# Infini-attention with a gated FFN on one core: a new instruction order, planned with turns for the readers of one PSUM bank

## The chip, the core and the metric

The kernel runs on one core of one Trainium2 chip. The core has five instruction streams that run side by side and wait for each other by semaphores: TensorE (PE in the profile; PEld is its weight load), VectorE (DVE), ScalarE (ACT), GpSimd (POOL) and SyncE (SP), which issues nearly all DMAs. Products of TensorE land in PSUM, which this kernel uses as eight banks of 128 x 512 floats. The metric is the device time of one execution in microseconds; shown are the median and the extremes of three runs, and one more execution that was profiled.

## What is computed

The input is 2048 tokens of width 512. There are 32 heads of width 16, and the tokens are four segments of 512. Cut to its core, the reference is:

```
x = A_x
h = x + A(layernorm(x))
out = h + B(layernorm(h))

A: q, k, v = x @ wq, x @ wk, x @ wv, per head
   for each of four segments s, in order:
       a_dot = softmax(qs ks^T * scale + causal mask) vs
       a_mem = phi(qs) M / (phi(qs) z + 1e-6),   phi(t) = t+1 if t > 0 else exp(t)
       o = g * a_mem + (1 - g) * a_dot,          g = sigmoid(beta)
       M += phi(ks)^T vs;  z += sum of phi(ks)
   return concat(o) @ wo
B: (gelu(x @ w_gate) * (x @ w_up)) @ w_down      # hidden width 1376
```

All of it is float32. TensorE gets each operand as a high part in a rounded format and the low rest, and forms three products (high x high, high x low, low x high); so almost every operand needs a copy (the high part) and a subtraction (the low part) on ACT, DVE or POOL before TensorE may use it.

## The kernel before

**Stages.** The attention runs in 16 units, each one segment and one group of eight heads. A unit normalises and transposes its segment (once per segment), projects q and k (L959, and L980 for the first unit), projects v (L1008, and L1021 for the first), moves q and k by DMA into the stacked tiles `stq` and `stk`, then runs a pass that finds each query's largest score (scores L1213 on PE, maxima L1223 on DVE), and a second pass that recomputes the scores transposed (L1271), takes exponentials (L1277 on ACT), masks them (L1285 on POOL) and multiplies by v (L1299). After the attention come the output projection (L1372, L1379), the second norm, and the FFN in two halves of 1024 tokens. FFN products (L1563) and most of the down projection (L1737) are done as seven block products in place of eight; the last hidden tiles of the second half go through a plain down projection, L1631, whose sums are added to the output rows (L1639 on DVE) and stored (L1644). What the seven-product part gives is transposed on DVE (L718), sent through the DRAM tensor `y_dram`, loaded again and added on POOL (L1775).

**What sets the order.** The kernel first records 5308 operations, each with an engine, a planned duration, the values it reads and the values it writes. `ORDER` is a written-out permutation of them. `Sched.run` goes through `ORDER` and emits each operation on its engine; the engines' own queues are therefore exactly the order of the list, and nothing is reordered later. Buffers (rows of `P2`, PSUM banks, operand slots of 128 x 2 x 512) are given out in the same walk: of the free buffers a value takes the one that by the planned times came free first. So the planned times choose which buffer a value gets, and through this which semaphore it waits for. Waits are put in by the framework from the tiles that the instructions really touch, not from the plan.

**The opening.** `ln1_first` (L876) loads the first segment's four row tiles (L882), takes statistics per tile (L891, L892), adds epsilon into a PSUM bank (L899), takes the root on ACT (L901), inverts (L906) and forms the shift (L907), applies both (L912 on DVE for even tiles, L916 on ACT for odd ones; the pages name tiles by buffer), transposes on PE (L921), and splits (L926 on ACT, L928 on DVE). It does so in two halves of two tiles, called the first half and the second half below. Before the first real transpose PE runs 14 small transposes of a unit matrix (L896). SP issues the loads of the first Wk and Wq (`split_weight`, L686), of Wv (`split_wv`, L703) and of the second segment's rows (L938). The low part of Wk is formed on POOL (L692), that of Wq on DVE (L695).

**The norms.** `layer_norm` (L726) has two ways to invert the root: a root on ACT (L797) with a reciprocal on DVE (L801, L802), and a series of DVE steps (L778), of which one reads a small tile `z` in SBUF twice.

**The end.** `geglu` (L1579) leaves the activated hidden tile in SBUF (`e`) or in a PSUM bank; for the last tiles its high part is taken by ACT (L1596) and its low part by POOL or DVE (L1599). `down` (L1617) cuts the last output tile of all into two halves of 256 columns, which have sums and stores of their own; the second half's store is issued by ACT.

## Time and profile before

| | before |
|---|---|
| median of 3 runs | 741.16 us (741.01 to 743.85) |
| profiled execution | 740.42 us |
| its span in the profile | 738.7 us |
| PE busy | 719.6 us of the span, 6442 instructions |
| DVE busy | 634.8 us, 1990 instructions |
| ACT busy | 534.0 us, 1138 instructions |
| POOL busy | 523.1 us, 815 instructions |
| granted TensorE clock | 1.00 |
| DMA queue of SP | 135.71 MB, packets take 63.6% of 16 engines' span |

The span is counted from the first to the last instruction of the program; 1.7 us of the execution lie around it. The profile lists idle time of each engine before a group of instructions and the instruction that ended it. Busy time of PE counts a matmul that waits inside PE's pipeline as busy, so a stretch with PE busy throughout can still hold short waits; these are then seen on PEld, whose loads wait for the operand or the bank.

### The profile page before, as it was taken

How to read it: one execution, taken by the hardware profiler on the slowest of the kernel's cores; microseconds unless marked ns; L12 is line 12 of the kernel's file. 1: busy time of each engine (PE TensorE's matmuls, PEld its weight loads, DVE VectorE, ACT ScalarE, POOL GpSimd, SP SyncE). 2: the span in 40 equal slices, each digit the busy share in tenths (PEclk: the TensorE clock that was granted, in tenths of full speed). 3: DMA queues.
4: the chain of work that ended last, by engine and by line, in shares of the span. 5: the costliest groups of instructions: out<-in, count | busy, mean ns of one | idle time of the engine just before them, and what ended most of it. 6: DMA issues, size and time to landing. Idle time of an engine off the chain costs nothing.

```text
span 738.7 us, 19243 instructions
## 1 busy us (share of the span) xinstructions
PE 719.6 (97%) x6442; PEld 570.6 (77%) x6442; DVE 634.8 (86%) x1990; ACT 534.0 (72%) x1138; POOL 523.1 (71%) x815
## 2 busy tenths in 40 slices
PE   6999999999999999999999999999999999999996
PEld 5877877777878787777666888888887778888885
DVE  6998889988988888898987665889999999779996
ACT  6789979798685878867867656978787665666341
POOL 6344253554553746778899899998999977698766
PEclk9999999999999999999999999999999999999999
DMA  7754537656666776887856267677574249756767
GB/s 256 204 144 109 131 99 191 183 142 174 170 157 168 193 202 190 210 237 202 212 189 211 74 198 234 214 238 216 185 219 142 71 127 269 247 180 204 220 173 248
DMA packets 100798, 137.32 MB, mean 186 GB/s; under 512 B 18028, under 2 KB 40732, under 8 KB 100700
## 3 DMA queue, kind: packets, MB, share of 16 engines
q1 hardware_dynamic: 100396, 135.71, 63.6%
q8 instruction: 51, 0.84, 0.5%
q10 hardware_dynamic: 304, 0.39, 0.2%
q14 instruction: 47, 0.39, 0.2%
HBM read 70.67 MB, written 39.26 MB: 149 GB/s over the span
## 4 chain that ended last, share of the span: by engine, by line
PE 67%; DVE 11%; issue 3%; POOL 2%; DMA 2%; ACT 2%; SPq 1%; ACTq 0%; DVEq 0%; POOLq 0%
PE bank L1563 23%; PE bank L959 8%; PE bank L1299 7%; PE bank L1737 7%; PE bank L1271 5%; PE bank L1213 4%; PE bank L1379 3%; PE bank L1372 3%; PE bank L1008 3%; DVE row L1748 2%; DVE aside L1223 2%; PE bank L1631 2%; DVE bank L1223 1%; PE bank L1181 1%; DMA t_dram<-row 1%
## 5 line engine op out<-in xcount | busy, mean ns | idle before, releaser
L1277 ACT ACTIVATE row<-bank 128x512 f32<-128x512 f32 x320 | 170.9, 608 | 24.8 <-PE bank L1271 20.3
L1285 POOL TENSOR_SCALAR_AFFINE_SELECT row<-row 128x256 f32<-128x256 f32 (+1 forms) x320 | 107.8, 364 | 96.1 <-ACT row L1277 95.0
L1223 DVE CUSTOM_DVE_ANT_0 aside<-bank,amask 128x256 f32<-128x256 f32 (+2 forms) x384 | 141.1, 419 | 12.4 <-PE bank L1213 6.7
L959 PE MATMUL bank<-slot,slot 64*128 64x512 f32 x720 | 113.5, 403 | 0.3 <-DVE nm L1223 0.2
L1563 PE MATMUL bank<-slot,slot 128*128 128x512 f32 (+1 forms) x366 | 97.3, 390 | 0.0
L1223 DVE CUSTOM_DVE_ANT_0 bank<-bank,amask 128x512 f32<-128x512 f32 x128 | 86.1, 710 | 10.5 <-PE bank L1213 7.5
L1271 PE MATMUL bank<-stq,stk 64*128 64x128 f32 (+3 forms) x512 | 82.1, 337 | 0.8 <-ACT row L1114 0.5
L1299 PE MATMUL bank<-row,vaug 128*32 128x512 f32 (+3 forms) x1024 | 79.0, 436 | 1.8 <-DVE nm L1223 1.2
L1213 PE MATMUL bank<-stk,stq 64*128 64x256 f32 (+3 forms) x512 | 78.9, 326 | 1.7 <-DVE nm L1223 1.1
L1563 PEld LDWEIGHTS bank<-slot,slot 128*128 128x128 f32 (+1 forms) x366 | 67.8, 186 | 15.8 <-ACT stq L1419 0.4
L1748 DVE TENSOR_TENSOR row<-row,bank 128x512 f32<-128x512 f32 x110 | 72.0, 677 | 7.1 <-PE bank L1737 5.6
L959 PEld LDWEIGHTS bank<-slot,slot 64*128 64x128 f32 x720 | 73.3, 185 | 6.0 <-DVE nm L1223 0.7
L1528 POOL TENSOR_TENSOR slot<-row,slot 128x512 fp32r<-128x512 f32 (+3 forms) x60 | 67.1, 1124 | 14.1 <-ACT slot L1526 14.0
L1271 PEld LDWEIGHTS bank<-stq,stk 64*128 64x128 f32 x512 | 55.5, 185 | 15.5 <-DVE nm L1223 3.7
L1213 PEld LDWEIGHTS bank<-stk,stq 64*128 64x128 f32 x512 | 56.1, 185 | 9.6 <-DVE nm L1223 2.4
L1737 PE MATMUL bank<-slot,half 128*128 128x512 f32 x234 | 61.7, 390 | 0.0
L1299 PEld LDWEIGHTS bank<-row,vaug 128*32 128x32 f32 x1024 | 30.0, 109 | 39.2 <-issue 34.1
L1008 PE MATMUL bank<-slot,slot 64*128 64x256 f32 x672 | 53.4, 284 | 0.0
L1570 ACT ACTIVATE vaug<-bank 128x512 f32<-128x512 f32 (+1 forms) x66 | 38.5, 591 | 18.6 <-PE bank L1563 18.5
L1737 PEld LDWEIGHTS bank<-slot,half 128*128 128x128 f32 x234 | 43.8, 188 | 9.6 <-DVE row L1748 0.4
L1223 DVE DVE_READ_ACCUMULATOR2_ANT nm<- 128x1 f32 x512 | 49.9, 97 | 0.0
L1008 PEld LDWEIGHTS bank<-slot,slot 64*128 64x128 f32 x672 | 48.7, 186 | 1.0 <-DVE mb L1138 0.2
(228 smaller groups left out, 1722.2 us busy)
## 6 DMA issues: line engine op xcount, KB each, us to landing
stq<-slot SPq DMA_DIRECT2D x96, 128.0 KB
stk<-slot SPq DMA_DIRECT2D x94, 128.0 KB
row<-x SPq DMA_DIRECT2D x32, 256.0 KB
pv_dram<-row SPq DMA_DIRECT2D x32, 256.0 KB
row<-r_dram SPq DMA_DIRECT2D x28, 256.0 KB
wd_dram<-half SPq DMA_DIRECT2D x28, 256.0 KB
half<-wd_dram SPq DMA_DIRECT2D x28, 256.0 KB
row<-wu SPq DMA_DIRECT2D x20, 256.0 KB
```

The costliest lines, as they stand in the source:

```text
L959: return nc.tensor.matmul(pm[i].t, w[i].t[rows_of(r), wi, dc * P:(dc + 1) * P], XT[s][dc].t[rows_of(r), xi, :], start=(dc, wi, xi, ph) == ...
L1008: return nc.tensor.matmul(pms[n].t[:, 256 * t:256 * t + 256], XT[s][dc].t[rows_of(r), xi, t0:t0 + P], whl[wi].t[rows_of(r), dc // 2, 256 * ...
L1213: nc.tensor.matmul(sa.t[:, c0:c0 + w], sq.t[own, p, i * P:(i + 1) * P], sk.t[own, p, 0:w], start=True, stop=True, tile_position=(64 * a, 0 ...
L1223: nc.vector.tensor_tensor_reduce(out=(sa.t[:, c0:c0 + w] if i > 2 else aside[:, turns[0]:turns[0] + w]), in0=sa.t[:, c0:c0 + w], in1=amask ...
L1271: nc.tensor.matmul(sc.t[:, c0:c0 + D - q0], sk.t[own, p, q0:q0 + P], sq.t[own, p, q0:D], start=True, stop=True, tile_position=(64 * a, 0), ...
L1277: act(w, prio, lambda sc=sc, e=e: nc.scalar.activation(e.t[:, :w], sc.t[:, :w], AF.Exp), [sc, vtab], [e])
L1285: nc.gpsimd.affine_select(v, v, pattern=pat + [[1, P]], compare_op=OP.is_ge, fill=0.0, base=0, channel_multiplier=-1)
L1299: nc.tensor.matmul(pv.t[32 * n:32 * n + 32, kb * P:D], va.t[:, 136 * kb + 17 * j:136 * kb + 17 * j + 32], e.t[:, lo:lo + D - kb * P], star ...
L1528: pool(0.14 + 2.13e-3 * (hi - lo), prio, lambda: nc.gpsimd.tensor_tensor(v.t[:, 1, :hi - lo], r.t[:, lo:hi], v.t[:, 0, :hi - lo].bitcast(F ...
L1563: nc.tensor.matmul(dst.t[:w], v.t[:, wi, c0 + j * w:c0 + (j + 1) * w], b[bk][j].t[:, xi, :], start=first and j == 0 and n == 0, stop=j == ...
L1737: nc.tensor.matmul(dst[u].t, ws[a].t[0][:, wi, P * u:P * u + P], h[bk].t[:, xi], start=first and m == 0, stop=m == 2, skip_group_check=True)
L1748: dve(D, prio, lambda u=u, acc=acc: nc.vector.tensor_tensor(acc.t, acc.t, src[u].t, op=OP.add), [src[u]], [acc])
```

## The change

The list `ORDER` is replaced whole: 5308 entries become 5309, for the operations are numbered anew. Its first line tells a reader nothing; the rows further down show what it does.

```diff
 ORDER = [
-    4, 6, 10, 76, 0, 1, 2, 5, 11, 9, 12, 7, 27, 13, 14, 8, 16, 18, 28, 100, 91, 92, 29, 15, 17, 88, 30, 31, 32, 34,
...
+    6, 4, 77, 10, 5, 11, 9, 13, 14, 15, 92, 93, 12, 8, 29, 17, 19, 16, 18, 98, 89, 99, 90, 7, 28, 91, 30, 20, 21, 31,
...
```

**The plan knows turns.** The pool of PSUM banks is marked, and in the planned times an ACT or DVE operation that reads a bank starts only after the other engine's last planned read of the same value. This changes planned times, hence which buffers come free first, and no instruction by itself. Planned sizes of loads (`kb`) and durations (`dur`) change too.

```diff
-    PD = PX = PYZ = PA = PB = PPV = Pool_(banks)
+    PD = PX = PYZ = PA = PB = PPV = Pool_(banks, turns=True)
...
+        o.reads = [v for v in ins if v.pool is not None and v.pool.turns] if eng in ("ACT", "DVE") else []
...
+            for v in o.reads:
+                for e, end in v.read.items():
+                    if e != o.eng:
+                        at = max(at, end + LAT[e][o.eng])
```

**Small operands go to PSUM.** In `ln1_first` and in the norms with a root, the root stays in the PSUM bank, a second reciprocal writes the inverse there as well, and the shift is formed from it. In the series, `z` is written to PSUM, copied once to SBUF, and the step that read `z` twice now reads one copy from each.

```diff
+        def third():
+            if scratch:
+                nc.vector.tensor_copy(z.t, z_())
+            nc.vector.scalar_tensor_tensor(u_(), z.t, -10.0 / 3.0, z_(), op0=OP.add, op1=OP.mult)
...
             def inv(two=two):
-                nc.vector.reciprocal(y.t[:, two], z.t[:, two])
-                nc.vector.scalar_tensor_tensor(b.t[:, two], mv.t[:, two, 0], -1.0, y.t[:, two], op0=OP.mult,
+                nc.vector.reciprocal(y.t[:, two], sc.t[:, two])
+                nc.vector.reciprocal(sc.t[:, two], sc.t[:, two])
+                nc.vector.scalar_tensor_tensor(b.t[:, two], mv.t[:, two, 0], -1.0, sc.t[:, two], op0=OP.mult,
                                                op1=OP.mult)
```

**The end.** Hidden tile 9 of the second half is left in a PSUM bank (`u_` or `g_`) in place of the SBUF tile `e`, and its split reads it there. The last output tile is no longer cut: one sum of 512 columns, one store, issued by SP.

```diff
+            if f == 9 and hh:
+                o = g_ if s else u_
...
-                parts = 2 if (p, fl, s, t) == (1, groups[-1], 1, 3) else 1
...
-                        n, q = 8 * p + 4 * s + t, nc.scalar if i else nc.sync
+                    dma(prio, lambda a=a, dst=dst: nc.sync.dma_start(dst, a.t), [a],
```

**Finer pieces.** The first unit's v projection is recorded as eight operations with one bank each in place of four with two (`plain(n, t, h)`); the unit transposes of the opening are two operations in place of one; the low part of Wv no longer waits for the second half of its high part; the loads of Wv no longer stand behind the norm in the plan. The matmuls and their number are the same but for the uncut tile.

**What moves: the loads of the opening.** On SP, the first loads of the program were, and are (`x` are token rows, the first four of which are the first segment):

```order
L882 DMA row_101<-x 128x512
L882 DMA row_104<-x 128x512
L882 DMA row_105<-x 128x512
L882 DMA row_106<-x 128x512
L686 DMA row_107<-wk 128x512
L686 DMA row_108<-wq 128x512
L938 DMA row_109<-x 128x512
L703 DMA row_111<-wv 128x512
```

```order
L897 DMA row_101<-x 128x512
L897 DMA row_102<-x 128x512
L695 DMA row_103<-wk 128x512
L897 DMA row_104<-x 128x512
L712 DMA row_105<-wv 128x512
L695 DMA row_106<-wq 128x512
L897 DMA row_107<-x 128x512
L956 DMA row_111<-x 128x512
```

Wk goes from fifth place to third, the first segment's third tile from third to fourth, its last tile from fourth to seventh; Wq stays sixth. On PE, twelve of the first unit's q and k products (L998, before L980) now stand ahead of the second half's transposes; before, all sixteen transposes came first.

**What moves: the first norm on DVE.** From the second tile's statistics on, DVE's rows of the opening were, and are (`bank` holds the root's small operands, `ln` are the small SBUF tiles):

```order
L891 BN_STATS bn_158<-row_104 128x6
L892 BN_AGGR mv_160<-bn_158 128x2
L899 TENSOR_SCALAR bank_66<-mv_160 128x2
L891 BN_STATS bn_158<-row_105 128x6
L892 BN_AGGR mv_160<-bn_158 128x2
L906 RECIPROCAL ln_163<-ln_162 128x2
L907 SCALAR_TENSOR_TENSOR ln_164<-mv_160,ln_163 128x2
L891 BN_STATS bn_158<-row_106 128x6
```

```order
L907 BN_STATS bn_158<-row_102 128x6
L908 BN_AGGR mv_160<-bn_158 128x2
L916 TENSOR_SCALAR bank_66<-mv_160 128x2
L923 RECIPROCAL ln_162<-bank_66 128x2
L924 RECIPROCAL bank_66<-bank_66 128x2
L925 SCALAR_TENSOR_TENSOR ln_163<-mv_160,bank_66 128x2
L907 BN_STATS bn_158<-row_104 128x6
L908 BN_AGGR mv_160<-bn_158 128x2
```

The first half's inverse and shift now stand ahead of the third tile's statistics, and there is one reciprocal more.

**What moves: the last rows of ACT.** Here `slot` and `stq` and `stk` are operands of the last down projection, `row` hidden tiles in SBUF; before and after:

```order
L1596 ACTIVATE slot_89<-row_124 128x512
L1596 ACTIVATE slot_78<-row_122 128x512
L1585 ACTIVATE row_127<-row_127 128x512
L1644 DMA out_dram<-row_112 128x256
L1596 ACTIVATE slot_73<-row_127 128x512
```

```order
L1618 ACTIVATE stk_91<-row_108 128x512
L1601 ACTIVATE row_114<-bank_69 128x512
L1618 ACTIVATE slot_88<-bank_68 128x512
L1605 ACTIVATE row_114<-row_114 128x512
L1618 ACTIVATE stk_94<-bank_72 128x512
```

The store of the half tile, which stood ahead of the last operand's high part, is gone from ACT, and the last two operands come from banks.

More of the change, by code (lines that the diff above doesn't have):

```diff
@@ L58, with __init__ @@
 ORDER = [
[271 rows of a table removed]
[271 rows of a table added]
 ]
 class Pool_:
-    def __init__(self, tiles, fifo=False, then=None):
+    def __init__(self, tiles, fifo=False, then=None, turns=False):
+        self.turns = turns
         self.free = [(0.0, i, t) for i, t in enumerate(tiles)]
@@ L391, in __init__ @@
         self.users = 0
+        self.read = {}
         self.until = 0.0
@@ L399 @@
     __slots__ = ("eng", "dur", "lat", "fn", "prio", "vals", "preds", "succ", "n", "ready", "idx", "head", "tail",
-                 "mode")
+                 "mode", "reads")
 LAT = {
@@ L482, in run @@
             free[o.eng] = end
+            for v in o.reads:
+                v.read[o.eng] = end
             if o.eng == "SP":
@@ L810, in layer_norm @@
             for f, ins, outs in steps:
-                dve(4, prio, f, ins, outs)
+                dve(200 if f is third and scratch else 4, prio, f, ins, outs)
         if off:
@@ L1014, in vproj, with plain @@
         parts = [(t, h) for t in range(2) for h in range(2)]
-        def plain(t, h):
-            for n in range(2):
-                for dc in (2 * h, 2 * h + 1):
-                    for i, (xi, wi) in enumerate(SPLIT):
-                        t0 = (2 * n + t) * P
-                        nc.tensor.matmul(
-                            pms[n].t[:, 256 * t:256 * t + 256], XT[s][dc].t[:, xi, t0:t0 + P],
-                            whl[wi].t[:, h, 256 * (dc % 2):256 * (dc % 2) + 256],
-                            start=dc == 0 and i == 0, stop=dc == ND - 1 and i == 2)
-        for t, h in parts if s == c == 0 else []:
-            pe(12 * mm(256), prio, lambda t=t, h=h: plain(t, h), [*whl, *xt(s, 2 * h), *xt(s, 2 * h + 1)], pms, acq=va)
+        def plain(n, t, h):
+            for dc in (2 * h, 2 * h + 1):
+                for i, (xi, wi) in enumerate(SPLIT):
+                    t0 = (2 * n + t) * P
+                    nc.tensor.matmul(
+                        pms[n].t[:, 256 * t:256 * t + 256], XT[s][dc].t[:, xi, t0:t0 + P],
+                        whl[wi].t[:, h, 256 * (dc % 2):256 * (dc % 2) + 256],
+                        start=dc == 0 and i == 0, stop=dc == ND - 1 and i == 2)
+        for n in range(2) if s == c == 0 else []:
+            for t, h in parts:
+                both = slice(2 * h, 2 * h + 2)
+                pe(6 * mm(256), prio, lambda n=n, t=t, h=h: plain(n, t, h), [*whl, *XH[n][both], *XLH[n][both]],
+                   [pms[n]], acq=[*XT[0][both]] + (va if (n, t, h) == (0, 0, 0) else []))
         if s or c:
@@ L1590, in geglu @@
             o = g_ if s and f % 2 and by7(p, f) else e
+            if f == 9 and hh:
+                o = g_ if s else u_
             dve(D, prio, lambda: nc.vector.scalar_tensor_tensor(
-                o.t[:w], r.t[:w], 0.5, u_.t[:w], op0=OP.mult, op1=OP.mult), [u_] if o is r else [u_, r], [o])
+                o.t[:w], r.t[:w], 0.5, u_.t[:w], op0=OP.mult, op1=OP.mult), [v for v in (u_, r) if v is not o], [o])
             HH[p, f, s] = hh or o
@@ L1620, in down, with dn @@
             for t in range(4):
-                parts = 2 if (p, fl, s, t) == (1, groups[-1], 1, 3) else 1
-                a, W_ = ACC[4 * s + t], D // parts
-                halves = [slice(i * W_, (i + 1) * W_) for i in range(parts)]
-                pms = [Val(PD) for _ in halves]
+                a = ACC[4 * s + t]
+                pm = Val(PD)
                 for f in fl:
-                    def dn(t=t, f=f, s=s, pm=None, cs=None):
+                    def dn(t=t, f=f, s=s, pm=pm):
                         w = FW[f]
```

86 lines of the change are left out of this document (42 added, 44 removed), and 540 rows, old and new, of the table ORDER.

## The prediction

> **What bounds the kernel now.** I read the page's first rows, then busy time by stretch, then who waited for whom, and last the timeline at the places where PE waits.
>
> ```profile
> PE 719.6 (97%) x6442; PEld 570.6 (77%) x6442; DVE 634.8 (86%) x1990; ACT 534.0 (72%) x1138; POOL 523.1 (71%) x815
> PE 67%; DVE 11%; issue 3%; POOL 2%; DMA 2%; ACT 2%; SPq 1%; ACTq 0%; DVEq 0%; POOLq 0%
> ```
>
> ```profile
> core 0: us, PE busy (x) PEld busy (x) DVE busy (x) ACT busy (x) POOL busy (x), PEclk, DMA share, GB/s
> 0.00:8.27 8.27, 3.15 (x15) 1.80 (x15) 3.72 (x12) 2.53 (x5) 4.77 (x17) 1.00 0.71 236
> 8.27:24.14 15.87, 14.14 (x112) 13.32 (x113) 13.07 (x38) 13.08 (x35) 11.32 (x20) 1.00 0.75 241
> 24.14:376.00 351.86, 346.79 (x4655) 270.88 (x4657) 310.88 (x1340) 283.01 (x637) 195.75 (x448) 1.00 0.66 175
> 376.00:390.00 14.00, 13.12 (x141) 7.72 (x137) 11.49 (x30) 11.52 (x24) 12.32 (x21) 1.00 0.47 155
> 390.00:560.00 170.00, 170.00 (x772) 137.82 (x769) 137.45 (x277) 124.53 (x257) 160.05 (x178) 1.00 0.65 201
> 560.00:580.00 20.00, 19.53 (x83) 14.74 (x82) 19.88 (x34) 14.84 (x31) 19.43 (x22) 1.00 0.35 103
> 580.00:720.00 140.00, 139.98 (x616) 114.12 (x615) 125.99 (x246) 81.23 (x151) 107.90 (x104) 1.00 0.64 193
> 720.00:738.70 18.70, 12.94 (x62) 10.21 (x60) 12.28 (x19) 3.23 (x6) 11.56 (x9) 0.99 0.75 248
> ```
>
> PE is the bound: 97% busy, 67% of the chain, and without a gap for 310 of the 330 us of FFN (390 to 720). The change leaves PE's work as it is, and the granted clock is already 1.00. So all it can win lies in five places: the opening up to the first scores at 24.14 (PE idle for 8.27 - 3.15 = 5.1 us, then 15.87 - 14.14 = 1.7 us), the attention (351.86 - 346.79 = 5.1 us idle, with more waits inside busy time), the second norm at 376 to 390 (0.9 us), the middle of the FFN (0.5 us) and the end (5.8 us, most of it draining). What the attention hides shows on the weight loads:
>
> ```profile
> PEld bank L1271 <- DVE nm L1223: 3.7, 12, 0.4
> PEld bank L1213 <- DVE nm L1223: 2.4, 6, 1.2
> PEld bank L1299 <- POOL row L1285: 1.8, 5, 0.5
> PEld bank L1271 <- ACT row L1277: 1.7, 6, 0.4
> ```
>
> These four (asked between 20 and 376 us) make 9.6 us. Each is a bank or a row that another engine has not left or made in time, so they depend on the order alone.
>
> **The end.** Before, the last products wait for the low part of the last operand:
>
> ```profile
> 723.98 8.69 POOL L1775 TENSOR_TENSOR row<-row,row 128x512 f32<-128x512 f32 x6
> ...
> 727.79 0.38 ACTq L1644 DMA_DIRECT2D out_dram<-row  x1
> 728.22 0.63 ACT L1596 ACTIVATE slot<-row 128x512 fp32r<-128x512 f32 x1 [4.13 <-DVE row L1639]
> 728.89 1.38 DVE L1599 TENSOR_TENSOR slot<-row,slot 128x512 fp32r<-128x512 f32 x1 [1.13 <-ACT slot L1596]
> 730.32 0.96 PE L1631 MATMUL bank<-stq,slot 128*128 128x512 f32 x3 [0.63 <-DVE slot L1599]
> 732.32 2.05 DVE L1639 TENSOR_TENSOR row<-row,bank 128x512 f32<-128x512 f32 x3 [0.26 <-PE bank L1631]
> ```
>
> The half tile's store sits in ACT's queue ahead of that operand's high part and holds it for 4.13 us. Without it ACT can start when its row is done, about 2 us earlier, and PE's wait of **0.63 us** goes. The uncut tile also saves one add and one store, but those overlap PE. Next to be late is POOL: six additions in 8.69 us, ending at 732.67, while the last three adds on DVE start at 732.32. In the new list POOL has eight such additions in a row at the end; at 8.69 / 6 = 1.45 us each that is 11.6 us, and they must start before 721.1 not to be late. Their rows come back from `y_dram` as before. I take -0.6 us, between -1.0 (POOL's additions also freed) and +0.7 (POOL late by half an addition).
>
> **The second norm.** Its series on DVE holds the transposes, and one step of it is long:
>
> ```profile
> 380.27 1.28 POOL L1340 TENSOR_TENSOR row<-row,row 128x512 f32<-128x512 f32 x1
> 380.41 1.17 DVE L778 SCALAR_TENSOR_TENSOR bank<-ln 128x4 f32<-128x4 f32 x1
> 381.62 0.16 DVE L778 SCALAR_TENSOR_TENSOR ln<-bank,ln 128x4 f32<-128x4 f32 x1
> 385.09 0.28 PE L831 MATMUL bank<-ident,row 64*128 64x64 f32 x2 [0.36 <-DVE row L822]
> ```
>
> A step on 128 x 4 numbers takes 0.16 us where one operand is a bank, and 1.17 us where both are SBUF and POOL is at work: it ends when POOL does. The change gives that step one operand from each and adds a copy of about 0.17. So 1.17 becomes 0.16 + 0.17: 0.8 us less on the chain that PE's transposes wait for. PE's idle time in this stretch is 0.9 us, so I take **-0.8**, between -0.9 and 0 (another norm step meets POOL).
>
> **The opening.** Both directions occur. The first half's inverse moves ahead of the third tile's statistics:
>
> ```profile
> 5.45 0.17 ACT L901 ACTIVATE ln<-bank 128x2 f32<-128x2 f32 x1 [2.12 <-DVE bank L899]
> 6.21 0.69 DVE L891 BATCH_NORM_STATS2 bn<-row 128x6 f32<-128x512 f32 x1 [0.79 <-DMA row<-x]
> 7.04 0.13 DVE L906 RECIPROCAL ln<-ln 128x2 f32<-128x2 f32 x1
> 7.21 0.16 DVE L907 SCALAR_TENSOR_TENSOR ln<-mv,ln 128x2 f32<-128x2 f32 x1
> 7.40 0.81 ACT L916 ACTIVATE row<-row,ln,ln 128x512 f32<-128x512 f32 x1 [1.78 <-DVE ln L907]
> ```
>
> The root is there at 5.62; the reciprocal could follow at about 5.7, so the shift is ready some 1.1 us earlier, less 0.17 for the new reciprocal. But ACT now takes Wk's high part in between. In the second half the shift takes 1.08 us beside POOL and will take 0.16:
>
> ```profile
> 8.82 1.27 POOL L692 TENSOR_TENSOR slot<-row,slot 128x512 fp32r<-128x512 f32 x1 [2.94 <-ACT ln L901]
> 9.02 1.08 DVE L907 SCALAR_TENSOR_TENSOR ln<-mv,ln 128x2 f32<-128x2 f32 x1
> 8.15 0.33 SPq L686 DMA_DIRECT2D row<-wk  x1
> 8.82 0.33 SPq L938 DMA_DIRECT2D row<-x  x1
> ```
>
> Against this, the first segment's last tile is now the seventh load. The third load had landed at 6.21 (the statistics above). SP holds eight loads; its issues at 8.15 and 8.82 wait for the sixth and the seventh, some 0.65 us apart. So the last tile lands near 8.8 instead of 6.9 (8.8 less three loads), and the second half's statistics, root and shift run some 1.0 us later even with the shorter shift (1.9 - 0.9). PE has cover for part of it: twelve products of 0.125 us (48 take 6.0 us, row below) now stand ahead of the second transposes.
>
> ```profile
> L980 PE MATMUL bank<-slot,slot 128*128 128x256 f32 x48 | 6.0, 285 | 0.1
> L1021 PE MATMUL bank<-slot,slot 128*128 128x256 f32 x48 | 5.9, 283 | 0.0
> ```
>
> That is 1.5 us of cover against 1.0 us of delay. I take **0**, between -1.1 (the first half's head start kept) and +1.9 (the late tile uncovered).
>
> **The attention.** Here only the order counts. The plan now holds back an ACT read of a bank while DVE reads it. The waits are real already:
>
> ```profile
> ACT row L990 <- DVE slot L1072: 3.3, 6, 0.9
> ```
>
> That is the idle time of ACT before its read of a projected bank (L990), ended by DVE's read of the same bank (L1072). ACT is not the bound, so these 3.3 us cost PE little. What the plan gains is truer times at which banks come free, the very thing PE's loads wait for in the 9.6 us above. I take **-1.5** of it, about a sixth. Nothing in the trace excludes that other waits replace these: the ends are -4.8 (half goes) and +4.8 (they grow by half). The middle of the FFN, 0.5 us idle, I take at -0.2.
>
> The Trainium skill, page "PSUM — Partial Sum Buffer", section "PSUM bank collisions raise a hardware error", says that two engines must not access one bank in the same quadrant at once, reads included, and that the scheduler adds a dependency between them. The trace agrees: the 3.3 us are such waits. By this rule the new plan removes no wait, since each of them stands in the program either way; then the attention's term is 0, which is the second rival.
> The page "SBUF — State Buffer", section "SBUF: two separate sides", says that a DVE operation with two SBUF inputs and a GpSimd operation that reads SBUF lock each other out for the whole instruction. The 1.17 and 1.08 us beside POOL agree. By it the two norm steps are cured for good, as in my sum.
>
> **The sum.** 740.42 - 0.6 - 0.8 + 0 - 1.5 - 0.2 = 737.3 us against the profiled execution. The median of the runs shown, 741.16, is 0.7 above that execution, so the forecast for a median is **738.0 us**.
>
> **Rivals.**
> 1. *The attention gains much.* If half of the 9.6 us goes (4.8 in place of 1.5), the time is 738.0 - 3.3 = 734.7. For it: the waits are many (29) and short, 0.3 us each, so a slightly truer plan reaches them. Against it: the old order was fitted to nearly the same plan.
> 2. *The turns are bookkeeping.* The semaphores stay and waits only move, so the attention and the FFN's middle give nothing, and the late tile costs 0.9 of its 1.9 us: 738.0 + 1.7 + 0.9 = 740.6. For it: PE in attention is busy for 346.79 of 351.86 us, little is left.
> 3. *Slower: the new order makes PE's loads wait longer for banks that the maxima (L1223) or exponentials (L1277) hold.* If the four rows grow by half, that is +4.8 in place of -1.5: 738.0 + 6.3 = 744.3. It decides from the point where they grow by more than the other terms save (0.6 + 0.8 + 0.2 = 1.6 us, a sixth of 9.6); beyond that the kernel is slower than before. For it: DVE is busy for 310.88 of 351.86 us there, so a maximum put a little late has no slack to catch up.
>
> **How the numbers follow.** Forecast 0.42 (its own range 736.0 to 739.8, from the ends of the opening and the small terms), rival one 0.27, rival two 0.19, rival three 0.12. The range 733.5 to 743.0 holds the first three whole but for rival one's lower end, and the nearer part of the third. A measurement of this kernel can tell about 0.5% from no change, that is 737.45 and 744.87. Faster by more: nearly all of rival one and a third of the forecast, 0.41. Slower by more: the upper half of rival three, 0.06. Within: 0.53.
>
> **What would show it.** In the changed kernel's timeline the end is right if the last L1650 products run without a wait of 0.5 us and POOL's eight additions end before the last adds begin. The norm is right if no step of the series takes over 0.5 us near 380. The opening is right if the first scores start within 1 us of 24.14. The attention is right if the four rows of weight-load waits sum to about 8 us; rival one says under 5, rival three over 14. The forecast is wrong if a stretch of the FFN that has PE full now shows idle time, since I priced none there.

## The result, and the profile after

| | before | after |
|---|---|---|
| median of 6 runs each, us | 741.09 (740.20 to 743.85) | 734.49 (732.84 to 737.15) |
| ratio, 95% interval | | 0.9902 (0.9883 to 0.9920) |
| profiled execution, us | 740.42 | 733.41 |
| its span, us | 738.7 | 731.7 |

The kernel became faster by 6.6 us in the medians and by 7.0 us between the two profiled executions. The direction and the range of the prediction hold the result; the size was forecast at 3.1 us, less than half. The page of the changed kernel (engines busy, then shares of the chain) reads:

```profile
PE 715.0 (98%) x6436; PEld 573.3 (78%) x6436; DVE 629.9 (86%) x1998; ACT 532.5 (73%) x1138; POOL 522.4 (71%) x815
PE 70%; DVE 5%; DMA 2%; issue 1%; POOL 1%; ACT 1%; SPq 0%; DVEq 0%; ACTq 0%; POOLq 0%
```

PE has become a larger share of the chain, 70% for 67%, and DVE a smaller one, 5% for 11%. The busy time by the same stretches as before:

```profile
core 0: us, PE busy (x) PEld busy (x) DVE busy (x) ACT busy (x) POOL busy (x), PEclk, DMA share, GB/s
...
24.14:376.00 351.86, 346.67 (x4702) 273.99 (x4700) 314.69 (x1353) 285.92 (x640) 199.03 (x451) 1.00 0.65 176
376.00:390.00 14.00, 13.76 (x138) 9.26 (x135) 9.50 (x26) 12.68 (x26) 13.17 (x27) 1.00 0.71 232
390.00:560.00 170.00, 169.63 (x745) 138.27 (x745) 139.50 (x283) 125.75 (x263) 159.87 (x174) 1.00 0.63 192
560.00:580.00 20.00, 20.00 (x89) 16.00 (x88) 18.97 (x32) 12.63 (x27) 19.13 (x21) 1.00 0.43 134
...
```

In the attention PE's busy time hardly differs (346.67 us for 346.79 of the same 351.86), yet 47 more products fit into it (4702 for 4655). What was saved there is not idle time of PE but waits inside its busy time. They are seen on the weight loads. The four rows of the prediction, and one that is new, for 20 to 376 us:

```profile
PEld bank L1291 <- DVE nm L1243: 3.5, 11, 0.5
PEld bank L1233 <- DVE nm L1243: 2.2, 7, 0.9
PEld bank L1233 <- ACT row L1297: 2.0, 4, 1.0
PEld bank L1319 <- POOL row L1305: 0.5, 2, 0.3
PEld bank L1291 <- ACT row L1297: 0.4, 1, 0.4
```

(L1291, L1233, L1319, L1243, L1297 and L1305 were L1271, L1213, L1299, L1223, L1277 and L1285.) The four fell from 9.6 to 6.6 us; the row of L1233 waiting for ACT, 2.0 us, was not there. Four rows are therefore a poor gauge. Summing *every* wait of the weight loads that the view gives, except those that it puts down to "issue", at stretches of the same work, gives a fuller one:

| stretch, us of before | before, us / waits | after, us / waits |
|---|---|---|
| 0 to 24 (opening) | 7.4 / 5 | 6.0 / 6 |
| 24 to 190 (attention) | 11.5 / 35 | 11.3 / 33 |
| 190 to 305 (attention) | 7.7 / 19 | 3.8 / 12 |
| 305 to 350 (attention) | 2.7 / 9 | 3.7 / 11 |
| 350 to 392 (end of attention, norm) | 6.5 / 20 | 5.5 / 15 |
| 392 to 545 (FFN) | 0.3 / 1 | 1.7 / 4 |
| 545 to 600 (FFN) | 2.4 / 5 | 0.4 / 2 |
| 600 to the end | 1.5 / 2 | 0.2 / 1 |
| sum | 40.0 / 96 | 32.6 / 84 |

The sum fell by 7.4 us, the span by 7.0. The sum shows where the waits went; it does not measure the gain. In half_before below it falls by 3 us where the span falls by 6.0, and the waits that the view puts down to "issue", left out here, fell as well, from 41 to 37 us. One stretch of the attention, 190 to 305 us, holds more than half of what the sum lost.

A second reading is used for all experiments: **PE's lead**. PE's work is the same in both kernels but for the uncut tile (every product is counted with about the shortest spacing that its shape shows in the trace), so one can ask when a given part of it has been started. The table gives the time at which a kernel has started that much work, less the time of before; negative is earlier. The columns are places of before: opening done, attention at 187, 303 and 371 us, past the second norm (400), FFN at 516, 578 and 718, and the span. All are single profiled executions; the kernels other than `after` are the experiments described below. How far an entry can be trusted shows in two places. `after` and `no_turns` turn out to be the same program, and their rows differ by up to 0.5 us. And the first column, which moves the start of every row, spreads more than that.

| kernel | 30 | 187 | 303 | 371 | 400 | 516 | 578 | 718 | span |
|---|---|---|---|---|---|---|---|---|---|
| after | -0.8 | 0.0 | -4.1 | -4.0 | -4.9 | -5.0 | -6.0 | -6.1 | -7.0 |
| no_turns | -0.6 | 0.5 | -3.8 | -4.1 | -5.0 | -5.1 | -6.4 | -6.5 | -7.4 |
| old_order | -0.8 | -0.9 | -0.7 | -0.6 | -0.8 | 0.4 | 0.4 | 0.4 | -0.5 |
| new_then_old | 0.0 | 0.9 | -3.4 | -3.7 | -4.2 | -3.5 | -3.5 | -3.5 | -4.8 |
| old_then_new | 0.9 | 0.8 | 0.3 | 0.4 | 2.0 | 2.1 | 0.4 | 0.3 | -0.1 |
| only_middle | -0.1 | 0.5 | 0.4 | 1.4 | 1.2 | 2.2 | 2.2 | 2.2 | 0.4 |
| middle_2 | -0.2 | 0.0 | -3.7 | -2.7 | -2.9 | -1.9 | -1.9 | -2.0 | -3.8 |
| late_new | -1.0 | -1.0 | -0.9 | -0.5 | -0.7 | 0.3 | 0.6 | 0.4 | -0.5 |
| uncut | -0.9 | -1.1 | -1.6 | -1.0 | -1.0 | -0.9 | -0.9 | -0.9 | -2.2 |
| z_sbuf | -0.8 | 0.3 | -3.2 | -3.9 | -4.8 | -5.1 | -6.1 | -6.2 | -6.5 |
| half_before | -0.7 | -5.4 | -6.7 | -8.0 | -6.2 | -5.6 | -5.6 | -5.6 | -6.0 |
| half_after | -1.1 | -4.0 | -6.5 | -7.7 | -8.3 | -8.6 | -10.1 | -10.2 | -10.5 |
| swaps | -0.8 | -0.1 | -3.8 | -4.5 | -5.4 | -5.5 | -7.1 | -7.2 | -8.0 |

For the changed kernel the row reads: attention -3.2 (from -0.8 to -4.0), second norm -0.9, FFN -1.2 (from -4.9 to -6.1), end -0.9. The attention's step is -3.1 to -3.7 in all five kernels that have the whole new list there with full scans, and -0.5 to 0.5 in the four with the old one, so it stands clear of the spread.

### The profile page after: what moved, and what is told of

Its sections match the earlier page's. It is cut to its first block, busy times and chain, and to the rows that moved or that the text cites. A ratio compares the mean times of both kernels' runs of the same rounds, so it can differ in the third digit from the quotient of the medians.

```text
span 731.7 us, 19207 instructions
## 1 busy us (share of the span) xinstructions
PE 715.0 (98%) x6436; PEld 573.3 (78%) x6436; DVE 629.9 (86%) x1998; ACT 532.5 (73%) x1138; POOL 522.4 (71%) x815
## 4 chain that ended last, share of the span: by engine, by line
PE 70%; DVE 5%; DMA 2%; issue 1%; POOL 1%; ACT 1%; SPq 0%; DVEq 0%; ACTq 0%; POOLq 0%
PE bank L1583 27%; PE bank L1751 11%; PE bank L1319 7%; PE bank L977 6%; PE bank L1291 4%; PE bank L1233 3%; PE bank L1392 3%; PE bank L1399 3%; PE bank L1650 2%; PE bank L1026 2%; DVE aside L1243 1%; PE bank L1201 1%; DVE bank L1243 1%; DMA row<-wdp 1%; DVE row L1654 1%
## 5 line engine op out<-in xcount | busy, mean ns | idle before, releaser
L1297 ACT ACTIVATE row<-bank 128x512 f32<-128x512 f32 x320 | 170.7, 611 | 28.5 <-PE bank L1291 23.4
L1305 POOL TENSOR_SCALAR_AFFINE_SELECT row<-row 128x256 f32<-128x256 f32 (+1 forms) x320 | 108.3, 366 | 88.0 <-ACT row L1297 75.6
L1243 DVE CUSTOM_DVE_ANT_0 aside<-bank,amask 128x384 f32<-128x384 f32 (+2 forms) x384 | 139.8, 419 | 10.0 <-PE bank L1233 4.8
L977 PE MATMUL bank<-slot,slot 64*128 64x512 f32 x720 | 111.4, 403 | 0.1
L1583 PE MATMUL bank<-slot,slot 128*128 128x512 f32 (+1 forms) x387 | 102.8, 391 | 0.4 <-ACT vaug L1590 0.4
L1243 DVE CUSTOM_DVE_ANT_0 bank<-bank,amask 128x512 f32<-128x512 f32 x128 | 86.4, 710 | 12.4 <-PE bank L1233 11.1
L1583 PEld LDWEIGHTS bank<-slot,slot 128*128 128x128 f32 (+1 forms) x387 | 71.7, 186 | 17.2 <-ACT vaug L1590 0.8
L1319 PE MATMUL bank<-row,vaug 128*32 128x512 f32 (+3 forms) x1024 | 78.7, 436 | 1.9 <-DVE nm L1243 1.4
L1291 PE MATMUL bank<-stq,stk 64*128 64x128 f32 (+3 forms) x512 | 79.4, 335 | 0.8 <-DVE mb L1158 0.2
L1233 PE MATMUL bank<-stk,stq 64*128 64x384 f32 (+3 forms) x512 | 76.0, 327 | 2.9 <-DMA stk<-slot 0.6
L1751 PE MATMUL bank<-slot,half 128*128 128x512 f32 x258 | 68.1, 390 | 0.0
L1548 POOL TENSOR_TENSOR slot<-row,slot 128x512 fp32r<-128x512 f32 (+3 forms) x52 | 60.5, 1170 | 6.7 <-ACT slot L1546 6.7
L1291 PEld LDWEIGHTS bank<-stq,stk 64*128 64x128 f32 x512 | 53.6, 185 | 13.1 <-DVE nm L1243 3.5
L1233 PEld LDWEIGHTS bank<-stk,stq 64*128 64x128 f32 x512 | 53.7, 185 | 12.4 <-DVE nm L1243 2.2
L1319 PEld LDWEIGHTS bank<-row,vaug 128*32 128x32 f32 x1024 | 31.7, 109 | 37.8 <-issue 31.5
L1751 PEld LDWEIGHTS bank<-slot,half 128*128 128x128 f32 x258 | 48.4, 188 | 10.4 <-DVE row L1608 0.3
L1243 DVE DVE_READ_ACCUMULATOR2_ANT nm<- 128x1 f32 x512 | 50.2, 98 | 0.0
```

What stands on the lines that cost most here:

```text
L977: return nc.tensor.matmul(pm[i].t, w[i].t[rows_of(r), wi, dc * P:(dc + 1) * P], XT[s][dc].t[rows_of(r), xi, :], start=(dc, wi, xi, ph) == ...
L1233: nc.tensor.matmul(sa.t[:, c0:c0 + w], sq.t[own, p, i * P:(i + 1) * P], sk.t[own, p, 0:w], start=True, stop=True, tile_position=(64 * a, 0 ...
L1243: nc.vector.tensor_tensor_reduce(out=(sa.t[:, c0:c0 + w] if i > 2 else aside[:, turns[0]:turns[0] + w]), in0=sa.t[:, c0:c0 + w], in1=amask ...
L1291: nc.tensor.matmul(sc.t[:, c0:c0 + D - q0], sk.t[own, p, q0:q0 + P], sq.t[own, p, q0:D], start=True, stop=True, tile_position=(64 * a, 0), ...
L1297: act(w, prio, lambda sc=sc, e=e: nc.scalar.activation(e.t[:, :w], sc.t[:, :w], AF.Exp), [sc, vtab], [e])
L1305: nc.gpsimd.affine_select(v, v, pattern=pat + [[1, P]], compare_op=OP.is_ge, fill=0.0, base=0, channel_multiplier=-1)
```

## Experiments: the list, the plan or the edits

Below, `new` is the list of the changed kernel, `old` that of before, renumbered for the changed program's operations. The kernels hold the resulting list written out; an entry that would stand ahead of its operands was moved just behind them (one in old_order, two in only_middle).

**old_order**: the changed program, the old list.

```diff
-ORDER = new
+ORDER = old
```

> The changed program with the list of before: its 5308 entries renumbered for the 5309 operations (the new pieces stand where the old whole stood), all other edits kept. Theory A, the gain is the order's: the time goes back to that of before, 739 to 743 us. Theory B, the small edits of the code carry it (the tile z in PSUM, the uncut last tile, truer buffers): 734 to 737 us. If the old list meets buffers that it was not fitted to, it may also come out above before, over 743.

Measured: 741.40 us, ratio 1.0012 (0.9997 to 1.0027). All edits of the code together, without the list, are worth nothing that can be measured. Theory B falls. The table shows two terms under this zero: 0.9 us are gained at the end, and 1.2 are lost between 400 and 516 us, to a single wait at 464 us that the kernel before does not have:

```profile
PEld bank L1763 <- DVE row L1420: 1.5, 1, 1.5
```

The same wait, 1.0 to 1.4 us, stands in new_then_old, only_middle, middle_2 and late_new, and one of 1.0 us in half_before, which has none of the edits. Its cause was not followed. The other half of the question, the new list without the edits, was run only for one edit (z_sbuf, below).

**no_turns**: the changed list, with the banks' pool no longer marked.

```diff
-    PD = PX = PYZ = PA = PB = PPV = Pool_(banks, turns=True)
+    PD = PX = PYZ = PA = PB = PPV = Pool_(banks)
```

> The changed kernel with its own list, but the pool of banks not marked, so that planned times, and with them the choice of buffers, know no turns. Theory A: the list alone sets the time, 733.5 to 736 us. Rival, the turns give better banks: 737 us or more.

Measured: 733.29 us, ratio 0.9905 (0.9888 to 0.9922), beside 0.9902 for the changed kernel. This could not come out otherwise. With the new list the marks change no buffer: the walk through `ORDER` gives every value the same bank, row and slot with and without them, and the two traces hold the same instructions on every engine, with the same semaphores. So no_turns is a second set of executions of the changed kernel. (With the old list the marks change 574 of the 2533 buffers that the walk gives out; that list in the changed program without marks was not run.) In the changed kernel the turns do nothing but through the list. Whether they helped to find it, no run shows.

**new_then_old** and **old_then_new**: the halves of the list, cut at about 379 us, in the second norm.

```diff
-ORDER = new
+ORDER = new[:3117] + [i for i in old if i not in new[:3117]]
```

```diff
-ORDER = new
+ORDER = old[:3117] + [i for i in new if i not in old[:3117]]
```

> The changed program; the new list up to its entry 3117 (opening and attention, to about 379 us), then the rest as the old list has it. The table of PE's loss by stretch gives 4.9 us of the gain to the stretches before 400 us and 2.1 to those behind. Theory A: 735 to 737.5 us. If the gain is the order's but sits in the FFN and the end: 739 to 741.

> The complement: the old list up to entry 3117, then the rest as the new list has it. Theory A: 738 to 740.5 us, so that this and the run before it together give the whole difference. If the gain sits in the FFN and the end: 734 to 736. If the sum of the two gains is far from 6.6 us, the halves are not independent (buffers handed over at the cut).

Measured: 736.49 us, ratio 0.9948 (0.9929 to 0.9967), and 740.50 us, ratio 1.0006 (0.9991 to 1.0020). The first is as theory A has it: opening, attention and the start of the second norm carry most of the gain. The second stands at the upper end of what was expected, and the two gains do not add up: 0.52% and -0.06% against 0.98% for both. The table of the lead shows why. In old_then_new the seam costs 1.6 us (0.4 at 371, 2.0 at 400), and the FFN then gains 1.7 (2.1 at 516, 0.4 at 578). So the FFN's part of the list works here, and its gain paid for the seam.

## Experiments: what holds the attention's gain

**only_middle**: the old list, with the new one's order between about 187 and 305 us. **middle_2**: the same with both cuts moved a little.

```diff
-ORDER = new
+ORDER = old[:1465]; ORDER += [i for i in new[:2417] if i not in ORDER]; ORDER += [i for i in old if i not in ORDER]
```

```diff
-ORDER = new
+ORDER = old[:1400]; ORDER += [i for i in new[:2412] if i not in ORDER]; ORDER += [i for i in old if i not in ORDER]
```

> The changed program with the old list, but between its entries 1465 and 2417 (about 187 to 305 us) the order of the new list. Summed over all waits of PE's weight loads, that stretch held 7.7 us before and 3.8 after, against 8.1 with the old list in the changed program. Theory A, the gain sits in the waits of this stretch: its loads wait for 4 to 5 us, and the time falls by 2.5 to 4 us below that of the old list (741.4): 737 to 739 us. Rival, the gain is the sum of small things all over the attention (97 fewer changes of PE between groups): under 1.5 us, 740 or more.

> As the run only_middle, but with the cuts at entries 1400 and 2412 in place of 1465 and 2417 (the first some 8 us earlier). There the stretch gained 2.4 us inside, and a wait of 2.0 us at the first seam (PE's L1264 on POOL's L1258) and 0.9 at the second took it back. If the seam's wait is an accident of the cut, it is gone or under 0.7 us here, and the time falls to 738.3 to 739.8. If the new stretch needs what the new list does before it, a wait of over 1 us stands at this seam too, and the time stays at 740.5 to 742.

Measured: only_middle 740.99 us, ratio 1.0002 (0.9980 to 1.0025), no gain, the time of its rival but not for the rival's reason; middle_2 736.83 us, ratio 0.9941 (0.9922 to 0.9960), more than was expected. PE's timeline at the first seam of only_middle, with the idle time ahead in brackets:

```profile
195.01 0.23 PE L1264 MATMUL bank<-ident,mm 64*32 64x64 f32 x2 [2.04 <-POOL mm L1258]
```

and of middle_2:

```profile
180.39 0.23 PE L1264 MATMUL bank<-ident,mm 64*32 64x64 f32 x2 [0.55 <-POOL mm L1258]
```

One wait at the seam ate the gain in only_middle (counted finer, its lead goes from 0.6 us at 187 to 2.7 at 196, and back to 0.2 at 300), and a cut some 65 entries earlier leaves it at 0.55 us. Inside the stretch middle_2 gains 3.7 us (0.0 at 187, -3.7 at 303), nearly the 4.1 of the whole new list; its second seam then gives back 1.0. The gain is in the order of this stretch, and a piece of an order works only when the engines arrive at its first entry about as they did where it was made.

What kind of waits are they? Between 30 and 400 us PE changes from one group of products to another some 880 times before and 790 times after. Take from each group's span the shortest spacing of its products, and what is left is its gap. Gaps under 0.15 us sum to about the same before and after; they move by about 1 us, up or down with the spacing that is taken as the shortest, so the fewer changes brought little. Gaps over 0.35 us became fewer, 28 with 15.7 us before and 19 with 11.1 after; with coarser groups, all products of one line together, 34 with 20.1 and 29 with 16.9. A few distinct waits are gone, and the largest of them shows the pattern. From PE's timeline of before:

```profile
192.66 0.96 PE L1008 MATMUL bank<-slot,slot 64*128 64x256 f32 x12
194.68 0.74 PE L1213 MATMUL bank<-stk,stq 64*128 64x256 f32 x8 [1.06 <-DVE nm L1223]
```

and from DVE's:

```profile
190.95 0.70 DVE L1223 CUSTOM_DVE_ANT_0 bank<-bank,amask 128x512 f32<-128x512 f32 x1
...
192.87 0.73 DVE L1223 CUSTOM_DVE_ANT_0 bank<-bank,amask 128x512 f32<-128x512 f32 x1
...
193.52 0.55 DVE L1223 CUSTOM_DVE_ANT_0 aside<-bank,amask 128x384 f32<-128x384 f32 x1
...
194.22 0.29 DVE L1223 CUSTOM_DVE_ANT_0 aside<-bank,amask 128x128 f32<-128x128 f32 x1
194.44 0.08 DVE L1223 DVE_READ_ACCUMULATOR2_ANT nm<- 128x1 f32 x1
```

DVE, without a pause, searches four full banks of scores for their maxima, 0.65 us from start to start, then three shorter ones. PE, which takes its products in the order of the list, is done with L1008 at 193.62 us and waits 1.06 us, until the last of the three is read. If such late reads are the cause, the new list should gain little where the scans are light.

**half_before** and **half_after**: both kernels with scans of at most 256 columns. The maximum over the rest of a wide tile is left out; PE's work and the lists stay.

```diff
-                        w = (i + 1) * P
+                        w = min(i + 1, 2) * P
```

> The kernel before, with the search for the largest score over at most 256 columns of a tile (it leaves out the rest of the 384 and 512 wide tiles); PE, ACT, POOL and the list are as before. Each scan of 512 columns then takes 0.35 instead of 0.65 us on DVE. Theory: in the attention PE waits because DVE, near 100% busy there, reads the scores' banks late; with light scans most of the loads' waits on L1223 go, PE's loss against its work falls by 4 to 8 us, and the time is 733 to 737. Rival: the waits come from the order whatever DVE's load: 739 to 741.

> The changed kernel with the same lighter scans. Theory: the new list has already taken a part of what DVE's lateness cost, so it gains less than the kernel before does, 1 to 4 us: 730.5 to 733.5, and the distance of the two kernels in the attention, 4.0 us of time with full scans, shrinks to 1 to 2.5. Rival, the new list's gain has nothing to do with DVE's lateness: the distance stays at about 4 us.

Measured: 734.05 us, ratio 0.9899 (0.9875 to 0.9922), and 728.25 us, ratio 0.9822 (0.9804 to 0.9839). DVE's busy time between 24.14 and 376 us, the last row of the view by stretch, in half_before (310.88 us in before):

```profile
sum 351.86, PE 348.19 PEld 270.59 DVE 274.69 ACT 289.48 POOL 203.42; mean PE 116.06 PEld 90.20 DVE 91.56 ACT 96.49 POOL 67.81
```

The first time lies in its range. The second does not: the changed kernel was to gain 1 to 4 us from light scans and gains about 6 (a ratio of 0.9822 for 0.9902), little less than the 7 to 8 of the kernel before. In the lead, with 36 us less on DVE the kernel before gains 7.3 us over the attention (-0.7 at 30, -8.0 at 371), though the loads' waits on the maxima, all rows from 24 to 392 us, fell only from 10.6 to 6.8 us, and not for the most part as expected. The changed kernel gains 3.7 beyond its own gain (-7.7 against -4.0). The distance of the two from 30 to 371 us is 3.2 us with full scans and none with light ones: half_after starts 0.4 us ahead and ends 0.3 behind.

The lead to 371 us speaks for DVE's late reads; the times do not bear it out, and how much of the new list's gain hangs on them is not settled. The distance in the medians is 5.8 us with light scans and 6.6 with full ones, which the intervals do not tell apart. Past the second norm (400 us) half_after is 2.1 us ahead of half_before, for 4.9 with full scans, because half_before loses 1.8 us in that norm. Between 187 and 303 us, where the new list's gain sits, it still gains 1.2 us more than the old one with light scans (4.1 with full ones). And that stretch is not the one where DVE is fullest. The kernel before, DVE's busy time being the third after the comma:

```profile
24.14:190.00 165.86, 164.07 (x2240) 128.88 (x2242) 146.55 (x644) 143.15 (x325) 72.90 (x188) 1.00 0.58 153
190.00:305.00 115.00, 112.60 (x1542) 88.39 (x1540) 96.59 (x416) 86.61 (x195) 67.29 (x149) 1.00 0.68 180
305.00:376.00 71.00, 70.12 (x880) 53.61 (x878) 67.73 (x282) 53.24 (x119) 55.56 (x112) 1.00 0.80 218
```

DVE is busy for 88, 84 and 95% of the three stretches, and the new list gains in the second alone. So at most a part of the list's advantage in the attention goes with DVE's load. Which waits make up the rest is open, and a mean load does not tell where a better order will gain. (Both lists were made for full scans; neither is fitted to the light ones.) Behind the attention half_after gains on half_before 2.4 us of lead in the second norm and 2.5 in the FFN.

## Experiments: the other terms

**uncut**: the kernel before, with the last output tile in one piece; its list is shorter by the four operations of one piece, and nothing else changes.

```diff
-                parts = 2 if (p, fl, s, t) == (1, groups[-1], 1, 3) else 1
+                parts = 1
```

> The kernel before with its own list, and one edit: the last output tile is not cut in two (its pieces stand where the later piece stood). As predicted: PE's wait of 0.63 us before the last products goes, 740.0 to 740.6 us. From the run with the old list, whose last products start 1.0 us earlier against its FFN than before: 739.6 to 740.2. Rival, POOL's last additions come late instead: 741 or more.

Measured: 739.61 us, ratio 0.9985 (0.9957 to 1.0014); too small for the interval. In the trace the lead grows from -0.9 at 718 us to -2.2 at the end, 1.3 us. (The same step is -0.4 in half_before, which still cuts the tile, and -0.3 to -1.8 in the kernels that do not, so its size is not settled by one execution.) That the wait is gone is plain in its timeline at the end:

```profile
724.14 7.42 PE L1631 MATMUL bank<-stq,slot 128*128 128x512 f32 x32
...
727.20 5.20 POOL L1775 TENSOR_TENSOR row<-row,row 128x512 f32<-128x512 f32 x4 [1.23 <-DMA row<-y_dram]
...
732.43 0.69 DVE L1639 TENSOR_TENSOR row<-row,bank 128x512 f32<-128x512 f32 x1 [0.54 <-POOL row L1775]
```

PE's last 32 products run without a wait, and POOL is what comes last instead: the last add waits 0.54 us for it.

**z_sbuf**: the changed kernel with the norm's third step on SBUF alone again.

```diff
-            return sc.t[:, 12:16] if scratch else z.t
+            return z.t
...
-            if scratch:
-                nc.vector.tensor_copy(z.t, z_())
```

> The changed kernel with its own list, but the series' third step reads the tile z in SBUF twice again, without the copy. As predicted: wherever it meets POOL it takes about 1.2 us, and PE's transposes of the second norm come up to 0.8 us later: 734.5 to 735.5 us. Rival, the new list hides it, for PE has other products there: the same as the changed kernel, 733.5 to 734.7, with the long step seen on DVE.

Measured: 733.59 us, ratio 0.9909 (0.9874 to 0.9943), the same as the changed kernel. The long step is back where it meets POOL, as in this norm of the FFN:

```profile
462.08 1.29 POOL L1548 TENSOR_TENSOR slot<-row,slot 128x512 fp32r<-128x512 f32 x1
...
462.26 1.15 DVE L799 SCALAR_TENSOR_TENSOR bank<-ln 128x4 f32<-128x4 f32 x1
```

but PE has products in hand there, and in the second norm the step happens to fall just as POOL ends, and takes 0.17 us. The reverse is in old_order, where the edit is made and the list is old (its line numbers are 12 above those of the changed kernel, so L849 is L837):

```profile
380.03 0.17 DVE L811 SCALAR_TENSOR_TENSOR bank<-ln,bank 128x4 f32<-128x4 f32 x1
...
381.04 3.67 DVE L849 TENSOR_SCALAR row<-row,mv,ln 128x512 f32<-128x512 f32 x4
...
381.19 1.54 POOL L1560 TENSOR_TENSOR slot<-row,slot 128x512 fp32r<-128x512 f32 x1
382.68 1.19 POOL L1560 TENSOR_TENSOR stq<-row,stq 128x384 fp32r<-128x384 f32 x1
```

The step is cured, 0.17 us, and most of the time that it saved is lost in the next operation: four applications of the norm take 3.67 us beside POOL's subtractions. They were slow in the kernel before too, beside the same subtractions:

```profile
382.42 3.06 DVE L822 TENSOR_SCALAR row<-row,mv,ln 128x512 f32<-128x512 f32 x4
```

So about 0.8 us are saved on the step and 0.6 lost behind it. In the changed kernel:

```profile
376.97 0.17 DVE L799 SCALAR_TENSOR_TENSOR bank<-ln,bank 128x4 f32<-128x4 f32 x1
...
378.43 1.96 DVE L837 TENSOR_SCALAR row<-row,mv,ln 128x512 f32<-128x512 f32 x4
```

The same four take 1.96 us, 1.1 less than before, where the new list has POOL's masks (L1305) beside them in place of the subtractions; in z_sbuf they take 1.99.

**late_new**: the old list up to about 555 us, then the new one.

```diff
-ORDER = new
+ORDER = old[:4261] + [i for i in new if i not in old[:4261]]
```

> The changed program with the old list up to its entry 4261 (about 555 us), then the rest as the new list has it. The loads' waits in the second half's first products (560 to 580 us) were 2.4 us with the old list and 0.4 with the new one. Theory A: they are 0.4 again, and the time is 1.5 to 2 us below that of the old list: 739.3 to 740 us. Rival, the wait only moves on to a later place of the FFN: 741 and a new wait of 1 us or more behind 580.

Measured: 739.77 us, ratio 0.9994 (0.9978 to 1.0011). The median lies in theory A's range, but the theory does not hold: the lead at the end is that of old_order, -0.5 us. No wait moved behind 580 us either. Before, the loads waited here for 2.4 us in five waits (545 to 600 us):

```profile
PEld bank L1563 <- DVE row L1748: 0.9, 2, 0.7
PEld bank L1737 <- DVE row L1748: 0.9, 2, 0.5
PEld bank L1737 <- ACT half L1685: 0.6, 1, 0.6
```

and in late_new one seam wait stands in their place:

```profile
PEld bank L1751 <- DVE row L1762: 2.1, 1, 2.1
```

In old_then_new, cut 176 us earlier, two waits of 0.2 us are left there. The FFN's gain is the list's as well, and the last part of the list alone did not bring it.

**swaps**: if a wait is a place in the order, moving one entry should remove it. Two were tried in the changed kernel.

```diff
-    ..., 1146, 1148, 1150, 1147, 1599, ...
+    ..., 1599, 1146, 1148, 1150, 1147, ...
...
-    ..., 3913, 3932, ...
+    ..., 3932, 3913, ...
```

> The changed kernel with two entries of the list moved. At about 141 us PE's L1233 of 384 columns waits 0.57 us for a bank that DVE is scanning, with a group of twelve L1026 ready behind it: that group goes first. At about 517 us ACT's L1590, for which PE's L1583 waits 0.37 us (its load 0.79), stands behind L1699, which waits 1.05 us for POOL: L1590 goes first. If such waits are places in the order, both go, and the time falls by 0.8 to 1.2 us against the changed kernel: ratio to before 0.9885 to 0.990. Rival, the wait only moves to the next PE group or the next ACT entry: no change, 0.990 to 0.991.

PE at 141 us, and ACT and PE at 517, in the changed kernel:

```profile
141.56 0.50 PE L1233 MATMUL bank<-stk,stq 64*128 64x384 f32 x4 [0.57 <-DVE nm L1243]
141.87 0.96 PE L1026 MATMUL bank<-slot,slot 64*128 64x256 f32 x12
...
516.34 0.42 ACT L1699 ACTIVATE half<-row 128x256 fp32r<-128x256 f32 x1 [1.05 <-POOL row L1693]
516.66 0.58 ACT L1590 ACTIVATE vaug<-bank 128x512 f32<-128x512 f32 x1
...
517.29 1.66 PE L1583 MATMUL bank<-slot,slot 128*128 128x512 f32 x6 [0.37 <-ACT vaug L1590]
```

and with the swaps:

```profile
141.12 0.89 PE L1026 MATMUL bank<-slot,slot 64*128 64x256 f32 x12
141.84 0.69 PE L1233 MATMUL bank<-stk,stq 64*128 64x384 f32 x8
...
514.84 0.59 ACT L1590 ACTIVATE vaug<-bank 128x512 f32<-128x512 f32 x1
515.51 0.42 ACT L1699 ACTIVATE half<-row 128x256 fp32r<-128x256 f32 x1
```

Both waits are gone. Measured: 732.94 us, ratio 0.9881 (0.9866 to 0.9896), below what was expected. The interval overlaps that of the changed kernel. The span, 730.7 us, is 1.0 us shorter than the changed kernel's 731.7 and 0.6 shorter than the 731.3 of no_turns, which is the same program; so a gain of this size is likely and not shown. It is the lowest median of the full computation here.

## Why the prediction was right in direction and wrong in size

Two steps failed. The attention's term was taken as a sixth of four rows of waits, -1.5 us, and measured -3.2; and PE's idle time was read as all there is to win in the FFN, -0.2 us, where -1.2 came. A third, the reason for the second norm, was wrong at the right size.

- **What bounds the kernel** was right: PE's work is unchanged, and the gain came in the five places named. It was 7.0 us in place of 3.1.
- **The end**, -0.6: measured -0.9 (old_order too), and -1.3 for the edit alone, each from one execution (uncut has the spread). The mechanism, a store in ACT's queue ahead of the last operand's high part, held. Of its marks, the last L1650 products do run without a wait, but POOL's additions end after the last adds begin; POOL is just in time, not early:

```profile
716.20 10.05 POOL L1789 TENSOR_TENSOR row<-row,row 128x512 f32<-128x512 f32 x8
...
724.40 2.74 DVE L1654 TENSOR_TENSOR row<-row,bank 128x512 f32<-128x512 f32 x4 [0.66 <-DMA out_dram<-row]
```

- **The second norm**, -0.8: the size is right (-0.9) and the reason is wrong. The step became short, as predicted, in all norms, yet old_order, which has it, gains 0.2 us there, and z_sbuf, which has it not, gains 0.9. The step that failed is "So 1.17 becomes 0.16 + 0.17: 0.8 us less on the chain": the next DVE operation, which already took 3.06 us beside POOL before, took 3.67. With the new list other POOL work stands beside them: that operation is 1.1 us shorter than before, and in z_sbuf the step is short there even without the edit. So the 0.9 come with the order, and that they equal the forecast is luck. By the Trainium skill, page "SBUF — State Buffer", section "SBUF: two separate sides", the prediction called the steps "cured for good". That holds for the steps; the rule is about neighbours in time, and says nothing of what the time saved is spent beside. Whether the 3.67 us in old_order is that rule at work one operation later is not shown: beside POOL's masks, which read and write rows of SBUF as well, the same four operations take 1.96 us.
- **The opening**, 0: the first scores start at 23.94 us for 24.14. The lead of -0.8 is no evidence of more. Executions with the old opening stand at 0, -0.9 and -0.7 in the program of before, and from -1.0 to 0.9 in the changed program; those with the new one from -1.1 to 0.0.
- **The attention**, -1.5: measured -3.2. This is the step that failed most. The term was mis-sized, at "about a sixth" of the 9.6 us of four rows. All rows of the loads' waits from 24 to 392 us make 28.4 us, and the new list took 4.1 of them. The four rows fell to 6.6, between the 8 of the forecast and the 5 of the first rival, but nothing in the profile pointed to a sixth; the weight came from the thought that the old order was fitted to nearly the same plan, which is no reading of the trace. What the profile did show, a DVE busy for 310.88 of 351.86 us on whose reads PE's banks hang, the prediction used only for the rival in which the kernel is slower. How much of the gain goes with that load half_before and half_after leave open; what is shown is that the gain lies in the order from 190 to 305 us (middle_2).
- "What the plan gains is truer times at which banks come free" falls: with the new list the turns change no bank (no_turns), so the gain is in the list alone. The wait of ACT for DVE's read of the same bank, 3.3 us before and 3.3 in old_order, whose plan knows turns, is with the new list

```profile
ACT row L1008 <- DVE slot L1092: 0.2, 1, 0.2
```

  and 0.5 us in no_turns, the same program. By the Trainium skill, page "PSUM — Partial Sum Buffer", section "PSUM bank collisions raise a hardware error", the program must hold such a wait either way; but a list can place the two readers so that it costs nothing, and the prediction's conclusion, that by this rule the attention's term is 0, did not follow. What these 3 us of ACT are worth to PE was not separated from the rest.
- **The FFN's middle**, -0.2: measured -1.2 for the whole FFN. The step that failed is reading PE's idle time there (0.5 us) in place of its loads' waits, 2.4 us from 545 to 600 and 1.5 behind. The forecast's own mark against itself also came true: from 390 to 560 us PE now idles for 0.37 us, behind the ACT entry that swaps moves.
- **The rivals**: the first (734.7 us) has the measured time, and that is partly luck: it asked for 4.8 us from the four rows, and of the 7.0 us less than half came in the attention, the rest in the opening, the norm, the FFN and the end. The second holds for the turns and not for the list. The third did not occur; its rows fell.

## What to carry to other kernels

Where the bounding engine is busy throughout, read the waits of its operand loads, all rows, summed by stage, ahead of its idle time: that sum moved by 7.4 us where the span moved by 7.0, while PE's idle time fell from 19.1 (738.7 - 719.6) to 16.7 us (731.7 - 715.0). It tells where to look, not what will be won (3 us for 6.0 in half_before). Much of this order's gain sat in a few distinct waits, and such a wait can be removed by asking what stands ready behind it: two moved entries removed both that they were aimed at. A piece of such an order cannot be judged by grafting it: seams cost up to 2 us here, as much as the piece brings. And an experiment on a plan is one only if the program that comes out differs.

## What the runs showed of the hardware that was not expected

- A DVE operation that was freed from a meeting with POOL let the next one lose the time: four L849 of 3.67 us in old_order, against 3.06 before and 1.96 in the changed kernel. With POOL's masks beside them (L1305) DVE keeps its 0.5 us each.
- The opening of one and the same list in the changed program differs by up to 1.9 us between executions (late_new and old_then_new, -1.0 and 0.9), so a single profile cannot settle a term of the opening under 2 us.
- In the attention the loads of L1299 (after, L1319) wait for about 30 us on nothing that the profile shows, 0.24 us each. The lists before and after:

```profile
PEld bank L1299 <- issue: 30.5, 126, 0.5
```

```profile
PEld bank L1319 <- issue: 29.5, 119, 0.5
```

This looks like four times the gain of this change, and no order tried here moved it. But in the kernel before 125 of the 140 such waits of the whole execution come right behind another load of L1299, and PE meanwhile can run its products without a pause that the view shows:

```profile
376.56 2.36 PE L1299 MATMUL bank<-row,vaug 128*32 128x512 f32 x32
...
377.01 0.13 PEld L1299 LDWEIGHTS bank<-row,vaug 128*32 128x32 f32 x4 [0.30 <-issue]
...
377.44 0.13 PEld L1299 LDWEIGHTS bank<-row,vaug 128*32 128x32 f32 x4 [0.30 <-issue]
```

So these waits are not time lost for PE by themselves, and no run shows that PE loses any by them.
